# Third stage in two product runs per block, half-block cosine, and wider spacing of the weight splits: retention, routed experts and a cosine feed-forward on one core

## The chip, the cores and the metric

One core of one Trainium2 chip runs the whole program. The metric is the device time of one execution in microseconds (us); lower is better.

## The reference

```python
# stage 1: retention over 8 batches, 8 heads, 576 positions, head size 64
ret = (scale * q @ k.T) * Dmat          # Dmat: gamma ** (row - column), lower triangle
x = (ret @ v) laid out as 4608 tokens x 512
# stage 2: 8 experts, one per token
e = argmax(x @ w_gate);  x = gate_w * (relu(x @ w1[e]) @ w2[e])    # 512 -> 1024 -> 512
# stage 3
h = x @ w_in                            # 512 -> 2048
out = (h * cos(h)) @ w_out              # 2048 -> 512
```

All inputs are random; `w_in` and `w_out` arrive as 64-bit floats and are turned into 32-bit ones on the chip.

## The kernel before

An fp32 product is made of three passes of rounded operands: each operand is split into a rounded part (a copy on ScalarE, ACT) and a rest (a subtraction on VectorE, DVE), and TensorE (PE) multiplies high by high, low by high and high by low. The program has three stages; every engine executes its instructions in the order in which the Python code emits them.

**Stage 2, the experts** (lines 595 to 881). Each of 8 experts has room for 616 tokens, in two halves of 256 and 360 columns. A half has 12 groups of matmuls: eight of the first layer (`layer1`, line 646, 12 matmuls each, evicted by ACT at line 649 and DVE at line 650) and four of the second (`layer2`, line 661, 24 matmuls each, evicted by ACT at line 663). Six PSUM banks (`hps`) turn over between them. After each group the loop calls `step_bg` (line 855), which advances a background generator by one or two turns (a turn ends at a `yield`), and `step_bgs`, which splits half a weight tile of the next expert. The background generator is `conv` (line 690): 32 tiles of the stage-3 weights are loaded, turned into 32-bit floats on DVE (seven turns, lines 700 to 712), split by `split_out` (line 681: an ACT copy into a buffer `cvo` of which there are two, a turn, a DVE subtraction, and two DMAs from GpSimd, POOL, to scratch memory in HBM) and stored. For `w_in`, four tiles together go to `combine` (line 724), which forms seven combined quarter matrices (a fast 2x2 scheme with seven products instead of eight) and splits and stores each (`keep`). There are four such combines. In the last expert the stage-3 weights are read back by `wide_unit` (eight loads of 1 MB) and `ws_load`, on the SP queue.

**Between the stages** stands `tc.If(late > 0)` (line 979) for overflowing experts, not taken here. All engines pass it together, and SP first waits for the DMAs that it has issued.

**Stage 3** (lines 987 to 1181). Nine tiles of 512 tokens; each tile has eight steps (a pair of 128-wide blocks of the hidden layer each), 72 steps `i` in all. A step has seven quarter products (`product`, line 1043, six matmuls of 256 columns each), whose inputs are seven combinations of input quarters (`turned`, line 1019, makes four of them; `enter`, lines 1026 and 1028, splits all seven). `decode` (lines 1057 and 1060) adds the products up to four quarters of h, `gate` (lines 1070 to 1083) turns each quarter of 128x256 into h cos h and splits it, and `down` (line 1113) multiplies by `w_out`: 24 matmuls of 512 columns per step, into four accumulators `acc`. After the last step of a tile `leave` evicts the four accumulators, alternately on DVE and ACT, into one of three row buffers, and POOL writes the rows out by an indirect DMA. The loop at line 1149 emits, per product, three or four matmuls of `down` of the step before (`PIECE`), so the 256- and 512-column matmuls alternate in seven pieces per step. `ahead` says at which points the next tile's inputs are loaded, turned and split.

Of the kernel before, what the change touches and what calls it, by code (L numbers as in the profile page):

```python
# [11 lines left out]
F32 = mybir.dt.float32  # L12
# [91 lines left out]
def attn_moe_kernel(ctx, tc, q, k, v, wg, w1, w2, win, wout, ctab, out):  # L104
# [490 lines left out]
    with ExitStack() as mctx:  # L595
# [128 lines left out]
        def combine(g, kc):  # L724
# [12 lines left out]
            yield from keep(4, n)  # L737
            sub(out=n, in0=n, in1=a11)
            yield
            yield from keep(1, n)  # L740
            yield from keep(2, a12)
            sub(out=a12, in0=a12, in1=n)
            yield
            yield from keep(6, a12)
# [80 lines left out]
        for e in range(E):  # L825
# [7 lines left out]
            for i, (hf, l, k) in enumerate(work):  # L833
# [21 lines left out]
                step_bg(2 if l == 2 or k % 2 == 1 else 1)  # L855
# [10 lines left out]
                elif i % 3 == 2:  # L866
                    wide_unit((0, 2, 1, 3)[i // 6], i // 3 % 2, nc.sync)
# [3 lines left out]
                if e + 1 == E and i in (17, 21):  # L871
                    ws_load(i // 21)
# [124 lines left out]
    near = yp.tile([P, 3, 2, 2, HT], F32R, name="near")  # L997
    ring += [near[:, n] for n in range(3)]
# [15 lines left out]
    def turned(T, n):  # L1014
# [4 lines left out]
        nc.vector.tensor_sub(out=t, in0=a, in1=b)  # L1019

    def enter(T, n, half=(0, 1)):
        src = [part(T, 0, 0), turn.get((T, 2)), part(T, 1, 0), turn.get((T, 3)), turn.get((T, 1)), turn.get((T, 4)),
               part(T, 1, 1)][n]
        t = enc[T, n] = ring[(NSLOT * T + n) % len(ring)]
        if 0 in half:
            nc.scalar.copy(out=t[:, 0], in_=src)
        if 1 in half:
            nc.vector.tensor_sub(out=t[:, 1], in0=src, in1=t[:, 0])

    BANK = (0, 1, 0, 1, 2, 3, 2)  # L1030
    SEEN = (0, 0, 1, 1, 0, 0, 1)
    bank = {}

    def product(i, s):
        T, q = i // NQ, i % NQ
        if not SEEN[s]:
            bank[i, BANK[s]] = psA.tile([P, 512], F32, tag="h", name="hps", bufs=4)
        o = bank[i, BANK[s]][:, :HT]
        u, x = units[2, i], enc[T, s]
        idx = 0  # L1040
        for kc in range(2):
            for a, bq in ((0, 0), (1, 0), (0, 1)):
                mm(out=o, lhsT=u[:, s, kc, a], rhs=x[:, bq, kc], start=(idx == 0 and not SEEN[s]), stop=(idx == 5),  # L1043
# [3 lines left out]
    h = {}  # L1047

    def decode(i, s):
        o = bank[i, BANK[s]][:, :HT]  # L1050
        if s == 2:
            h[i, 0, 0] = o
            return
        t = gp.tile([P, HT], F32, tag=f"d{s}", name="part", bufs=1 if s < 4 else 2)
        h[i, s] = t
        if s == 0:
            nc.scalar.copy(out=t, in_=o)  # L1057
            return
# [151 lines left out]
```

## Time and profile before

| | before |
|---|---|
| median of 3 runs | 1511.27 us (1510.29 to 1511.37) |
| the profiled execution | 1513.19 us, span 1511.4 us |
| PE matmul busy | 1444.5 us (96%) |
| DVE busy, ACT busy | 986.7 us (65%), 776.4 us (51%) |
| mean granted TensorE clock | 0.98 |
| stage 1 / stage 2 / stage 3 start | 0 / about 235 us / about 722 us |

The profile shows one execution: busy time of each engine, what ended each idle time, a time line, and for any stretch the busy time and the granted clock. PE is busy nearly throughout, so time is lost where PE waits, where its clock is lowered, and in the spacing of matmuls that follow one another without a wait. A busy matmul's duration includes its latency; the spacing is read from start to start.

### The profile page before, as it was taken

Reading aid. Unit: us, or ns where it says so; the run is one execution under the profiler, and the core shown is the slowest. Engines: PE = TensorE matmul, PEld = TensorE weight load, DVE = VectorE, ACT = ScalarE, POOL = GpSimd, SP = SyncE. Lnnn points to the kernel's source line nnn. Section 1 sums busy time; section 2 is a strip of 40 time slices with the busy share of each in tenths; the row PEclk is TensorE's granted clock in tenths of the full one; section 3 lists DMA queues with packets and bytes.
Section 4 is the critical chain, followed back from the end, with each engine's and each line's share of the span. In section 5 each row is a group of like instructions: output and inputs, shape, how many; then the busy total and the mean of one; then the engine's idle time right before and its main releaser. Section 6 shows DMA issues by size and latency. Waiting matters only on the chain.

```text
span 1511.4 us, 29804 instructions
## 1 busy us (share of the span) xinstructions
PE 1444.5 (96%) x11591; PEld 1330.9 (88%) x11591; DVE 986.7 (65%) x2321; ACT 776.4 (51%) x1911; POOL 223.0 (15%) x335
## 2 busy tenths in 40 slices
PE   8999979989999998999699999999999999999998
PEld 7888868989999998999698898989898898988887
DVE  3677666576766666741676766767677676767665
ACT  2344423434444534532466666666666665656654
POOL 3242532303210412210001001010100001010101
PEclk9999988999999999999799999999999999999999
DMA  9898936567665767766445555464646455555542
GB/s 189 207 218 213 221 99 178 184 190 230 199 212 181 231 196 223 227 208 242 151 175 216 183 194 207 163 242 156 249 152 225 173 204 196 190 209 189 190 180 77
DMA packets 179938, 293.48 MB, mean 194 GB/s; under 512 B 120676, under 2 KB 129328, under 8 KB 169552
## 3 DMA queue, kind: packets, MB, share of 16 engines
q1 hardware_dynamic: 166672, 248.92, 52.0%
q0 software_dynamic: 13120, 42.61, 8.4%
q8 instruction: 92, 1.51, 0.4%
q14 instruction: 54, 0.44, 0.1%
HBM read 239.43 MB, written 52.06 MB: 193 GB/s over the span
## 4 chain that ended last, share of the span: by engine, by line
PE 29%; issue 15%; ACT 3%; DMA 3%; DVE 2%; POOL 0%; POOLq 0%; DVEq 0%; ACTq 0%
PE acc L1113 15%; PE hps L1043 14%; DMA out_dram<-orow,perm 3%; ACT sa L1074 1%; ACT sa L1075 1%; ACT ka L1070 0%; ACT orow L1095 0%; DVE sa L1072 0%; ACT gh L1081 0%; POOL out_dram L1097 0%; DVE sa L1077 0%; DVE gl L1083 0%; DVE orow L1093 0%; ACT part L1057 0%; DVE turn L1019 0%
## 5 line engine op out<-in xcount | busy, mean ns | idle before, releaser
L1113 PE MATMUL acc<-wunit,gh 128*128 128x512 f32 x1152 | 395.4, 395 | 0.0
L1043 PEld LDWEIGHTS hps<-far,wquad 128*128 128x128 f32 x2160 | 306.2, 190 | 39.4 <-ACT part L1057 10.1
L1043 PE MATMUL hps<-far,wquad 128*128 128x256 f32 x2160 | 317.4, 283 | 5.0 <-ACT part L1057 4.9
L1060 DVE TENSOR_TENSOR part<-hps,part 128x256 f32<-128x256 f32 x360 | 152.2, 423 | 120.0 <-PE hps L1043 115.3
L1113 PEld LDWEIGHTS acc<-wunit,gh 128*128 128x128 f32 x1152 | 208.1, 189 | 23.3
L646 PE MATMUL hps<-xT,wunit 128*128 128x360 f32 (+1 forms) x1536 | 223.1, 306 | 4.7 <-DVE hl L650 4.7
L1113 PE MATMUL acc<-wunit,gl 128*128 128x512 f32 x576 | 227.4, 395 | 0.0
L646 PEld LDWEIGHTS hps<-xT,wunit 128*128 128x128 f32 x1536 | 220.2, 190 | 5.8 <-DVE hl L650 5.4
L661 PE MATMUL hps<-hh,wunit 128*128 128x360 f32 (+1 forms) x1024 | 223.6, 310 | 0.9 <-ACT hh L649 0.8
L1074 ACT ACTIVATE sa<-sa 128x256 f32<-128x256 f32 x288 | 120.5, 418 | 181.3 <-DVE sa L1072 181.3
L661 PEld LDWEIGHTS hps<-hh,wunit 128*128 128x128 f32 x1024 | 171.7, 192 | 1.3 <-ACT hh L649 1.3
L661 PE MATMUL hps<-hl,wunit 128*128 128x360 f32 (+1 forms) x512 | 158.4, 309 | 5.6 <-DVE hl L650 5.6
L1081 ACT CAST gh<-sa 128x256 fp32r<-128x256 f32 x288 | 117.1, 407 | 77.9 <-DVE sa L1077 77.9
L1097 POOL DMA_INDIRECT out_dram<-orow,perm x36 | 35.1, 974 | 801.9 <-DVE orow L1093 547.3
L1043 PEld LDWEIGHTS hps<-near,wquad 128*128 128x128 f32 x864 | 123.2, 191 | 28.8 <-ACT part L1057 9.9
L1083 DVE TENSOR_TENSOR gl<-sa,gh 128x256 fp32r<-128x256 f32 x288 | 121.4, 421 | 34.5 <-ACT gh L1081 25.4
L1043 PE MATMUL hps<-near,wquad 128*128 128x256 f32 x864 | 128.5, 285 | 14.6 <-ACT part L1057 7.7
L777 DVE TENSOR_TENSOR wunit<-wst,wunit 128x512 fp32r<-128x512 f32 x112 | 75.7, 686 | 79.8 <-ACT wunit L776 79.7
L1077 DVE SCALAR_TENSOR_TENSOR sa<-sa,part 128x256 f32<-128x256 f32 x216 | 91.9, 425 | 53.2 <-ACT sa L1075 46.0
L1075 ACT ACTIVATE sa<-sa 128x256 f32<-128x256 f32 x288 | 120.3, 418 | 9.2
L1113 PEld LDWEIGHTS acc<-wunit,gl 128*128 128x128 f32 x576 | 109.3, 190 | 10.2
L661 PEld LDWEIGHTS hps<-hl,wunit 128*128 128x128 f32 x512 | 98.3, 192 | 8.4 <-DVE hl L650 8.4
(178 smaller groups left out, 1815.6 us busy)
## 6 DMA issues: line engine op xcount, KB each, us to landing
wquad<-ws SPq DMA_DIRECT2D x72, 1792.0 KB, 7.4
wst<-in_moe_w_dram SPq DMA_DIRECT2D x64, 512.0 KB, 5.2
ws<-cvo POOLq DMA_DIRECT2D x56, 256.0 KB, 4.5
ldq<-in_q_dram SPq DMA_DIRECT2D x32, 256.0 KB, 4.6
ldk<-in_k_dram SPq DMA_DIRECT2D x32, 256.0 KB, 5.3
ldv<-in_v_dram SPq DMA_DIRECT2D x32, 256.0 KB, 5.3
xd<-xs SPq DMA_DIRECT2D x32, 256.0 KB, 3.0
cvw<-in_moe_w_in_dram SPq DMA_DIRECT2D x16, 512.0 KB, 4.8
```

The lines of the kernel that those rows point to most:

```text
L646: mm(out=ph[:, :n], lhsT=u[:, a, kc, f0:f0 + P], rhs=t[:, bq, kc, :n], start=(idx == 0), stop=(idx == 11))
L661: mm(out=py[:, :n], lhsT=u[:, w], rhs=t[:, :n], start=(fc == 0 and g == 0), stop=(fc == 7 and g == 2))
L777: nc.vector.tensor_sub(out=u[:, 1, 2 * g + c], in0=s[:, c], in1=u[:, 0, 2 * g + c])
L1043: mm(out=o, lhsT=u[:, s, kc, a], rhs=x[:, bq, kc], start=(idx == 0 and not SEEN[s]), stop=(idx == 5), skip_group_check=True)
L1060: nc.vector.tensor_add(out=t, in0=o, in1=h[i, other])
L1074: nc.scalar.activation(out=sa, in_=sa, func=AF.Sin, scale=math.pi)
L1075: nc.scalar.activation(out=sa, in_=sa, func=AF.Square, scale=math.sqrt(2.0))
L1077: nc.vector.scalar_tensor_tensor(out=sa, in0=sa, scalar=-1.0, in1=x, op0=ALU.add, op1=ALU.mult)
L1081: nc.scalar.copy(out=gh, in_=sa)
L1083: nc.vector.tensor_sub(out=gl, in0=sa, in1=gh)
L1097: ins = nc.gpsimd.indirect_dma_start(out=out[:, :], out_offset=bass.IndirectOffsetOnAxis(ap=perm[:, k:k + 1], axis=0), in_=o, in_offset=None)
L1113: mm(out=acc2[T][c], lhsT=t[:, c % 2 * P:(c % 2 + 1) * P], rhs=u[:, w, fc % 4], start=(q == 0 and fh == 0 and n == 0 and w == 0), stop=(q ...
```

## The change

Five edits in two stages.

```diff
@@ stage 2: combine and the background turns
             def keep(k, x):
                 yield from split_out(x, ...)
+                yield
+                yield
...
-                step_bg(2 if l == 2 or k % 2 == 1 else 1)
+                step_bg(4 if l == 2 else 1)
...
-                elif i % 3 == 2:
+                elif i % 3 == 0:
                     wide_unit((0, 2, 1, 3)[i // 6], i // 3 % 2, nc.sync)
...
-                if e + 1 == E and i in (17, 21):
-                    ws_load(i // 21)
+                if e + 1 == E and i in (16, 20):
+                    ws_load(i // 20)
@@ stage 3: inputs
-    near = yp.tile([P, 3, 2, 2, HT], F32R, name="near")
+    near = yp.tile([P, 5, 2, 2, HT], F32R, name="near")
-        nc.vector.tensor_sub(out=t, in0=a, in1=b)
+        (eng or nc.vector).tensor_tensor(out=t, in0=a, in1=b, op=ALU.subtract)
...
-    turned(0, 1)
...
+    turned(0, 1, nc.gpsimd)
...
+    turned(0, 2, nc.gpsimd)
...
+    turned(0, 3, nc.gpsimd)
...
+    turned(0, 4, nc.gpsimd)
@@ stage 3: sums and cosine, two quarters at a time
+    def decode_a(i):
...
+        nc.scalar.copy(out=p1, in_=x[:, :HT])
+        nc.vector.tensor_add(out=u2, in0=y[:, :HT], in1=p1)
+        nc.vector.tensor_add(out=u3, in0=z[:, HT:], in1=u2)
+
+    def decode_b(i):
...
+        nc.scalar.copy(out=t[:, 0], in_=x[:, :HT])
+        nc.vector.tensor_add(out=t[:, 1], in0=x[:, HT:], in1=u3)
+        nc.vector.tensor_add(out=p1, in0=y[:, :HT], in1=p1)
+        nc.vector.tensor_add(out=t[:, 2:4], in0=z.rearrange("p (a t) -> p a t", a=2),
+                             in1=p1.unsqueeze(1).to_broadcast([P, 2, HT]))
...
-        ka = gp.tile([P, HT], I32, tag="ka", name="ka", bufs=3)
+        ka = gp.tile([P, 2, HT], I32, tag="ka", name="ka", bufs=2)
@@ stage 3: the loop
+        if i < NALL:
+            for n in range(4):
+                product(i, n)
+            decode_a(i)
+        advance()
+        more(i, 1)
+        if i >= 2:
+            down(i - 2, 1)
+        advance()
+        more(i, 2)
+        if i < NALL:
+            for n in range(4, NSLOT):
+                product(i, n)
+            decode_b(i)
+        advance()
+        if i < NALL:
+            active.append(((i, 0), gate(i, 0)))
+        more(i, 3)
         if i + 2 < NALL:
             ws_load(i + 2)
+        if 1 <= i <= NALL:
+            down(i - 1, 0)
+        advance()
+        if i < NALL:
+            active.append(((i, 1), gate(i, 1)))
+        more(i, 4)
```

`advance` moves every active `gate` by two of its six turns; a `gate` now works on a pair of quarters (128x512 per instruction), and `down(i, half)` has the 12 matmuls of half the columns. `turned` takes an engine; for the first tile it is GpSimd. The seven quarter matrices and inputs are renumbered, so that four products run first and three second; three PSUM banks hold a step instead of four. A step's matmuls are the same in number and shape.

In the first of the four combines ACT is the engine that is waited for. `L684` is the copy into a `cvo` buffer, `L776` the split of the next expert's weights (`L778` after), `L663` and `L649` the evictions of the second and the first layer. Before:

```order
L649 ACTIVATE hh<-hps 128x360 x2
L684 CAST cvo<-cvn 128x512
L776 CAST wunit<-wst 128x512
L631 CAST xT<-tp 128x4x128 x2
L663 COPY yev<-hps 128x360
L684 CAST cvo<-cvn 128x512
L684 CAST cvo<-cvm 128x512
L776 CAST wunit<-wst 128x512
L663 COPY yev<-hps 128x360
L684 CAST cvo<-cvm 128x512
L663 COPY yev<-hps 128x360
L684 CAST cvo<-cvm 128x512 x2
```

The change, at the end of the same combine:

```order
L663 COPY yev<-hps 128x360
L684 CAST cvo<-cvm 128x512 x2
L778 CAST wunit<-wst 128x512 x3
...
L649 ACTIVATE hh<-hps 128x256
L618 ACTIVATE xrow<-xrow,sgate 128x512
L649 ACTIVATE hh<-hps 128x256
L618 ACTIVATE xrow<-xrow,sgate 104x512
L649 ACTIVATE hh<-hps 128x256
L684 CAST cvo<-cvm 128x512
```

The seven copies into the two buffers reach from the first layer of one half into the first layer of the next, where they took one second layer and its edges before.

On SP, in the last expert, the loads of `w_out` (`L785`, after `L787`) stand between the stores of the second layer (`L665`). Before, up to the branch:

```order
L665 DMA ydT<-yev 128x360
L790 DMA wquad<-ws_74 128x3584
L665 ISA
L665 DMA ydT<-yev 128x360
L665 ISA
L665 DMA ydT<-yev 128x360
L785 DMA wunit<-wd_73 128x2048
L979 COMPARE_AND_BRANCH
```

The change:

```order
L792 DMA wquad<-ws_74 128x3584
L665 ISA
L665 DMA ydT<-yev 128x360
L787 DMA wunit<-wd_73 128x2048
L665 ISA
L665 DMA ydT<-yev 128x360
L665 ISA
L665 DMA ydT<-yev 128x360
L981 COMPARE_AND_BRANCH
```

The last 1 MB load is issued two groups earlier, and the last DMA ahead of the branch is a store.

In stage 3, at the end of a tile, ACT in the change (`L1098` evicts an accumulator, `L1084` rounds a pair of quarters, `L1053` copies the first product, `L1073` to `L1078` are the cosine):

```order
L1098 ACTIVATE orow<-acc_10713 128x512
L1073 ACTIVATE ka<-quad 128x512
L1053 COPY part<-hps 128x256
L1077 ACTIVATE sa<-sa 128x512
L1078 ACTIVATE sa<-sa 128x512
L1073 ACTIVATE ka<-quad 128x512
L1098 ACTIVATE orow<-acc_10773 128x512
L1084 CAST gh<-sa 128x512
L1077 ACTIVATE sa<-sa 128x512
```

The fourth accumulator's eviction now stands right ahead of the rounding that the next run of `down` needs; before, the copy of the first product stood four narrow instructions behind the second eviction, and twelve behind the fourth.

## Rows read from the trace of the kernel before

**Rows 1.** Stage 2 by half experts: stretch, length, engines' busy us, clock, DMA, GB/s.

```profile
449.10:481.70 32.60, 32.60 (x202) 32.58 (x201) 20.32 (x39) 12.96 (x26) 3.58 (x4) 1.00 0.61 199
481.70:505.80 24.10, 24.10 (x206) 23.94 (x205) 18.55 (x35) 12.22 (x27) 6.51 (x8) 1.00 0.56 168
294.00:327.20 33.20, 27.74 (x205) 26.51 (x204) 22.39 (x44) 13.02 (x29) 7.85 (x9) 0.90 0.69 214
359.80:392.00 32.20, 27.62 (x207) 26.61 (x206) 22.06 (x44) 13.44 (x30) 8.36 (x11) 0.89 0.67 232
563.50:601.80 38.30, 33.95 (x202) 32.49 (x201) 22.94 (x43) 15.86 (x32) 11.44 (x15) 1.00 0.76 241
```

**Rows 2.** Waits of the whole run: who waits for whom, us, times, longest.

```profile
ACT cvo L684 <- DMA ws<-cvo: 39.3, 17, 5.0
```

**Rows 3.** DMA issues: queue, count, KB each, median us from issue to landing.

```profile
ws<-cvo POOLq DMA_DIRECT2D x56, 256.0 KB, 4.5
```

**Rows 4.** Time line of the fourth combine: start, us, engine, line, what [idle before <-releaser].

```profile
571.64 1.49 POOL L688 DMA_DIRECT2D ws<-cvo  x2 [1.24 <-ACT cvo L684]
...
576.39 0.62 ACT L684 CAST cvo<-cvm 128x512 fp32r<-128x512 f32 x1 [5.04 <-DMA ws<-cvo]
...
578.75 0.92 PE L646 MATMUL hps<-xT,wunit 128*128 128x360 f32 x4 [3.12 <-DVE hl L650]
```

**Rows 5.** Time line of SP ahead of stage 3.

```profile
715.62 0.34 SPq L665 DMA_DIRECT2D ydT<-yev  x1
716.13 0.33 SPq L785 DMA_DIRECT2D wunit<-wd  x1
```

**Rows 6.** SP's own waits between 690 and 760 us.

```profile
SPq L979 <- SPq L979: 5.1, 4, 3.4
```

**Rows 7.** Time line: first instructions of ACT and DVE in stage 3.

```profile
722.19 0.62 ACT L1026 CAST near<-yfirst 128x512 fp32r<-128x512 f32 x1 [6.59 <-SPq L979]
722.30 0.69 DVE L1019 TENSOR_TENSOR turn<-yfirst 128x512 f32<-128x512 f32 x1 [22.01 <-SPq L979]
```

**Rows 8.** First 23 us of stage 3: PE and weight loads of L1043, then of L1113.

```profile
722.80:746.08 23.28, 15.05 (x78) 13.72 (x78) 0.68 0.39 126
722.80:746.08 23.28, 1.84 (x6) 1.52 (x7) 0.68 0.39 126
```

**Rows 9.** POOL's subtractions and products of two inputs, by shape, and one in the time line.

```profile
L423 POOL TENSOR_TENSOR hot<-hot,ge 128x200 f32<-128x200 f32 x7 | 7.5, 1077 | 0.6
...
L423 POOL TENSOR_TENSOR hot<-hot,ge 128x80 f32<-128x80 f32 x1 | 0.4, 356 | 0.1
...
205.72 0.61 POOL L423 TENSOR_TENSOR hot<-hot,ge 128x200 f32<-128x200 f32 x1
```

**Rows 10.** Two steps of stage 3, between tiles: the first undisturbed, the second not.

```profile
982.06:992.61 10.55, 10.55 (x67) 9.50 (x67) 6.42 (x16) 5.96 (x17) 0.00 (x0) 1.00 0.75 275
992.61:1003.91 11.30, 10.81 (x67) 9.41 (x66) 7.07 (x19) 6.76 (x19) 4.24 (x8) 1.00 0.72 254
```

**Rows 11.** Waits of the whole run: PE on ACT's copy of the first product.

```profile
PE hps L1043 <- ACT part L1057: 12.6, 17, 3.5
```

**Rows 12.** Time line: a tile's first row store, the weight load, the fourth eviction.

```profile
992.61 11.64 SPq L790 DMA_DIRECT2D wquad<-ws  x2
...
992.64 0.97 POOL L1097 DMA_INDIRECT out_dram<-orow,perm  x1 [75.63 <-DVE orow L1093]
...
1000.86 0.60 ACT L1095 ACTIVATE orow<-acc 128x512 f32<-128x512 f32 x1 [2.08 <-PE hps L1043]
```

**Rows 13.** Time line of PE: twelve narrow matmuls, a piece of three, the tail.

```profile
735.76 1.60 PE L1043 MATMUL hps<-near,wquad 128*128 128x256 f32 x12
...
1002.31 0.40 PE L1113 MATMUL acc<-wunit,gh 128*128 128x512 f32 x1
...
1003.01 0.88 PE L1043 MATMUL hps<-far,wquad 128*128 128x256 f32 x6
...
1498.52 0.39 PE L1113 MATMUL acc<-wunit,gl 128*128 128x512 f32 x1
...
1500.56 0.39 PE L1113 MATMUL acc<-wunit,gl 128*128 128x512 f32 x1
```

More of the change, by code (lines that the diff above doesn't have):

```diff
@@ L996, in attn_moe_kernel @@
     ring = []
-    near = yp.tile([P, 3, 2, 2, HT], F32R, name="near")
-    ring += [near[:, n] for n in range(3)]
+    near = yp.tile([P, 5, 2, 2, HT], F32R, name="near")
+    ring += [near[:, n] for n in range(5)]
     for m in range(2):
@@ L1100, in leave, with down @@
         disjoint(ins.ins, "out")
-    def down(i):
+    def down(i, half):
         T, q = i // NQ, i % NQ
-        for c in range(4):
+        if q == 0 and half == 0:
+            acc2[T] = {}
+        pair = G.pop((i, half))
+        for c in (2 * half, 2 * half + 1):
+            if q == 0:
+                acc2[T][c] = psA.tile([P, DM], F32, tag=f"acc{c}", name=f"acc{c}")
             for fh in range(2):
@@ L1109, in down @@
                 for n, w in ((0, 0), (0, 1), (1, 0)):
-                    if q == 0 and c == 0 and fh == 0 and n == 0 and w == 0:
-                        acc2[T] = [psA.tile([P, DM], F32, tag=f"acc{k}", name=f"acc{k}") for k in range(4)]
-                    t = G[i, fh, c // 2][n]
-                    mm(out=acc2[T][c], lhsT=t[:, c % 2 * P:(c % 2 + 1) * P], rhs=u[:, w, fc % 4],
+                    mm(out=acc2[T][c], lhsT=pair[n][:, fh, c % 2 * P:(c % 2 + 1) * P], rhs=u[:, w, fc % 4],
                        start=(q == 0 and fh == 0 and n == 0 and w == 0), stop=(q == NQ - 1 and fh == 1 and n == 1))
-                    if q == NQ - 1 and fh == 1 and n == 1:
-                        leave(T, c)
-                    yield
-        for k in ((0, 0), (0, 1), (1, 0), (1, 1)):
-            del G[(i,) + k]
+            if q == NQ - 1:
+                leave(T, c)
     NB = NT // P
@@ new lines, in attn_moe_kernel, with advance @@
+    turned(0, 4, nc.gpsimd)
+    for n in (2, 3, 5):
+        enter(0, n)
+    ahead = {(0, 2): [raw_load], (1, 2): [turned, 1], (1, 4): [turned, 2], (2, 2): [turned, 3], (2, 4): [turned, 4],
+             (3, 2): [enter, 0], (3, 4): [enter, 1], (4, 2): [enter, 2], (4, 4): [enter, 3], (5, 2): [enter, 4],
+             (5, 4): [enter, 5], (7, 3): [enter, 6]}
+    active = []
+    def advance():
+        for _, g in active:
+            next(g)
+        for _, g in active:
+            next(g)
+        active[:] = [(k, g) for k, g in active if k not in G]
@@ new lines, in more @@
+    def more(i, point):
+        T, q = i // NQ, i % NQ
+        if T + 1 < NTILE and (q, point) in ahead:
+            f = ahead[q, point]
+            f[0](T + 1, *f[1:])
+    for i in range(NALL + 2):
+        if i < NALL:
[16 more added lines that the diff above has]
+        more(i, 3)
```

117 lines of the change are left out of this document (34 added, 83 removed).

## The prediction

> **What bounds the kernel.** I read the page's busy times first: PE is busy 96% of the span, so a gain has to come from PE's gaps, its clock or its spacing. The windows view by half experts shows where stage 2 loses: an undisturbed half takes 24.1 us (256 columns) or 32.6 us (360 columns), three others take 33.2, 32.2 and 38.3 us for the same matmuls, two of them with the granted clock at 0.90 and 0.89, so partly at the lower level of 1.2 GHz [rows 1]. That is 9.1 + 8.1 + 5.7 = 22.9 us. The view of waits names what is late there: ACT waits 39.3 us in 17 pieces until the stores of the split weights have freed a `cvo` buffer [rows 2]. The time line shows such a piece: ACT stands 5.04 us ahead of a copy, the evictions behind it are late, and PE, out of PSUM banks, waits 3.12 us [rows 4]. Stage 3 is PE from end to end: an undisturbed step takes 10.55 us with PE busy all of it [rows 10]. It loses time at its start [rows 7, 8] and at the end of each tile [rows 10, 11].
>
> **Stage 2: the splits.** Before, a combine is 11 turns (four sums, seven copies), and a half expert gives 20 turns (12 in its first layer, 8 in its second), so the seven splits are asked for in about half a half, 12 to 16 us. A buffer is taken for the copy 0.62, the subtraction 0.69, as another of the same width [rows 7], two POOL issues 1.49 [rows 4] and the landing 4.5 us [rows 3]: 7.3 us. Two buffers give a split per 3.65 us, seven in 25 us. The missing 10 us is what ACT stands still per combine: 39.3 / 4 = 9.8. After, a combine is 11 + 14 = 25 turns and a half gives 8 + 16 = 24, so the seven splits are asked for in about one half, 24 to 33 us. Demand meets supply. Within that, a second layer takes 16 turns, 5.3 splits, in 12 to 16 us and wants 19: ACT will still stand 3 to 4 us there. What covers that is the second layer itself: one short eviction per group and six PSUM banks. If that cover fails, the three slow halves come back in part. DVE gets four turns at once in a second layer (sixteen of up to 0.69 [rows 7], with the other splits and the transposed inputs more than a 12 us layer holds); it may run 2 to 3 us late into a first layer that has the banks to bear it. I take 21.5 of the 22.9 us as gained. The bounds: all of it, 23, and 8, if the landing under load is nearer 7 us than 4.5.
>
> **The branch.** The last 1 MB load is issued at 716.13 [rows 5], and SP waits at the branch, 3.4 us in its longest piece [rows 6], before ACT starts at 722.19 [rows 7]. With that load two groups of the second layer earlier the last thing in flight is the store of 715.62 [rows 5]; the 3.4 us piece goes: **-3.4 us**. It is nothing if another load lands as late, at best a little more.
>
> **The first step.** The first 84 matmuls of stage 3 (78 narrow, 6 wide) take 23.3 us [rows 8], where the steady spacing (below) would need 78 x 0.119 + 6 x 0.2325 = 10.7; 12.6 us are lost, to ACT and DVE preparing the inputs and to a clock of 0.68. Now POOL makes the four turned inputs, one after the other. Its price for 128x512: by the undisturbed row 0.61 at 200 columns and 0.356 at 80, so 2.1 ns a column, 1.26 us; by the mean 1.077 of all seven [rows 9], 6 ns a column, 2.95 us. The rows with the larger time are those that a DVE instruction with two SBUF inputs overlaps, and they are longer by about that overlap. I take 1.3 us each plus the DVE subtractions that fall into it (0.69 each, three in the first, one in each other), so the four are ready 3.4, 5.4, 7.5 and 9.5 us after the release. The last split and the copy of the first product follow ACT's order: 10.5 us. Then 18 narrow matmuls at the low level, 256 columns at 1.2 GHz or 0.213 us each: the first step ends 14.3 us after the release, 13.7 after the first matmul, 8.7 over its 5.0 at full rate. From there I find no stall: the second step has 42 more products before the first `down`. So 12.6 becomes 8.7 or a little more: **-3.5 us**. Bounds: -5 (clock up earlier), +3 (2.95 us each). The Trainium skill (GPSIMD Engine Reference, sections 1 and 4.1) speaks against this edit: elementwise work with two inputs belongs on VectorE, GpSimd being about 2x slower and sharing SBUF interfaces with it. The trace agrees on both counts (0.61 at 200 columns, 1.077 with overlap); by its 4497 ns for 2048 columns a turn would cost an estimated 1.1 us, and the sum would be the same within 1 us.
>
> **The tile ends.** At eight tile changes ACT's copy of the first product comes late behind the evictions: 17 waits, 12.6 us, of which 6.0 in the first step, so 15 of 0.44 us [rows 11], each with a restart. A disturbed step is 0.75 us longer [rows 10]. Between 6.6 (idle alone) and 15 x 0.75 = 11.3 I take 9 us. After, that copy has a run of 12 wide matmuls to hide behind, but the fourth eviction now stands ahead of the rounding for the next `down`, and it waits for the tile's first row store, which took 8.2 us (992.64 to 1000.86) beside a weight load issued in the same instant [rows 12]. Take t = 0 at the end of the first half of `down`. PE then has 24 narrow matmuls (to 2.85), 12 wide (to 5.65) and 18 narrow (to 7.8). The tile's first accumulator is done at -1.4 and its store starts near -0.2; the weight load, released by the narrow run before, starts at -2.8. So the store starts 2.6 us behind the load instead of with it, and I expect it done near 6. The fourth accumulator is ready at 5.65, its eviction ends near 6.7, the rounding near 7.4, and PE wants that at 7.8; where the store is a little later, PE waits. A stall of 0.3 us on average, 2.5 in all: **-6.5 us**. Bounds: -9, and +4 if the store takes its 8.2 us (1.65 us at each end).
>
> **The spacing.** Six narrow products take 0.71 us, 0.1185 each; in a piece of three the wide ones take (1003.01 - 1002.31) / 3 = 0.233, and in the tail, with nothing between, (1500.56 - 1498.52) / 9 = 0.2267 [rows 13]. By the step, (10.55 - 42 x 0.1185) / 24 = 0.232 [rows 10]. So 24 wide matmuls in seven pieces cost 0.14 us more than in one; with two pieces 2/7 of it stays: -0.10 us, 72 times, -7. Long narrow runs cost (1.60 - 0.28) / 11 = 0.120 [rows 13], 42 x 0.0010 x 72 = +3. I take **-4 us**, between -7 and +3. The Trainium skill (TensorE: Matmul & The Clock Gate, Back-to-back issue gap) gives a warm matmul N/2.4 + 2.5 ns alone, whatever stands beside it: then this term is 0. The trace shows 0.2267 and 0.233 for the same shape, so neighbours count.
>
> **The pair width.** ACT and DVE work per step falls (a 128x512 instruction takes 0.60 [rows 12] and 0.69 [rows 7], two of 128x256 about 0.8), which is worth nothing, since PE is the bound. What it must not do is come late: see the third rival.
>
> **The sum.** -21.5 - 3.4 - 3.5 - 6.5 - 4 = -38.9. The profiled execution took 1513.2 us, 1.9 over the median: 1474.3 by profile, **1472.4 us** by the median.
>
> **Rivals.**
> First, the splits still hold ACT: a landing of 7 us makes 9.8 us per buffer, 34 us for seven splits, more than a half. DMA at 0.67 to 0.76 in the slow halves [rows 1] speaks for it, the longer stretch against. Stage 2 then gives 8: 1486 us.
> Second, the fourth eviction: the store takes as long as before, PE waits 1.65 us per tile end, +4 instead of -6.5: 1483 us. The weight load's head start speaks against it.
> Third, slower: the pairs come late in every step. A pair's chain starts at the fourth product's end, 2.85 us after t = 0, and takes a narrow sum (under 0.69), a DVE pass 0.69, the rounding 0.60 and the rest 0.69, so with handoffs it ends near 5.9; PE wants the rest at 8.3, two wide matmuls into its run. That leaves 2.4 us. If the queues ahead of it on ACT and DVE eat that and 0.54 us more, the 38.9 us are gone; 1 us over gives 72 - 38.9 = +33: 1544 us. DVE and ACT at about 60% in a step [rows 10] speak against it.
> Fourth, spacing follows the shape alone (the page's rule): the term is 0, 1476 us.
> Fifth, the change doesn't do what it says: some other copy or load holds SP and ACT as now, and only the tile ends and spacing are left, -10: 1501 us.
>
> **How the numbers follow.** The forecast's own case 0.55, with the fourth rival 0.2 inside the same range; the first 0.1, the second 0.08, the third 0.03, the fifth 0.04. The range takes the forecast's bounds (-23 - 3.4 - 5 - 9 - 7 = -47, 1464) a little widened, 1462, up to just over the first rival, 1488. A measurement of this kernel can tell about 0.2%, 3 us. Faster 0.95; same 0.02 and slower 0.03 come from the third rival and part of the fifth.
>
> **What would show it.** ACT's wait for stored splits falls from 39.3 to under 15 us, and every half expert but the first takes under 25 or 34 us. The first product of stage 3 starts about 3.9 us after SP issues its last store instead of 7.2. POOL's turns take 1.3 to 3.4 us. No PE wait on the copy of the first product after the second step; waits at tile ends, if any, on the rounding `gh`. Wide matmuls at 0.228 on average. I am wrong if slow halves remain, if PE waits once per step, or if a step is over 10.55 us.

## The result, and the profile after

The changed kernel takes 1468.8 us (median of 4 runs, 1467.5 to 1470.0) against 1511.3 us of the kernel before beside it: a ratio of 0.970, interval 0.966 to 0.975. The profiled execution took 1467.5 us, its span is 1465.7 us against 1511.4 us. Forecast were 1472.4 us, in a range of 1462 to 1488 us.

The stages below compare one traced execution of each kernel. That of the kernel before was 1.9 us over its median, that of the changed kernel 1.3 us under, so the traces are 45.7 us apart where the medians are 42.5.

By stage, from first and last matmuls (us; "first two steps" are part of stage 3, which includes the spacing and the tile ends):

| | before | after | difference | forecast |
|---|---|---|---|---|
| start of stage 2 | 235.5 | 235.2 | -0.3 | 0 |
| stage 2 | 479.6 | 453.6 | -26.0 | -21.5 |
| last product of stage 2 to first of stage 3 | 7.80 | 3.76 | -4.0 | -3.4 |
| stage 3, all | 782.9 | 766.1 | -16.7 | -14.0 |
| its first two steps | 24.86 | 20.50 | -4.4 | -3.5 |
| over the median step at 8 tile ends | 10.9 | 0.5 | -10.4 | -6.5 |
| median step | 10.55 | 10.52 | -2 over 70 steps | -4 |
| behind the last matmul | 5.7 | 7.0 | +1.3 | 0 |

Both kernels have 84 narrow matmuls in their first two steps, the changed one 12 wide ones with them and the kernel before 10.

Stage 2 by half experts, the columns as in [rows 1]: the first half, one that was slow before (294.0 to 327.2 there) with the next, and a late pair.

```profile
235.20:260.90 25.70, 25.70 (x205) 25.48 (x205) 21.80 (x54) 9.79 (x22) 4.83 (x4) 0.93 0.64 197
...
293.50:317.50 24.00, 24.00 (x207) 24.00 (x206) 17.66 (x35) 12.61 (x28) 7.57 (x9) 1.00 0.80 257
317.50:350.10 32.60, 32.60 (x203) 32.58 (x202) 22.01 (x40) 13.98 (x28) 6.97 (x8) 1.00 0.58 177
519.80:543.70 23.90, 23.90 (x205) 23.90 (x205) 18.65 (x35) 12.32 (x27) 4.89 (x6) 1.00 0.57 178
543.70:576.30 32.60, 32.60 (x202) 32.58 (x201) 19.48 (x35) 15.42 (x31) 12.37 (x16) 1.00 0.76 243
```

PE is busy in every half from end to end, also where the DMA engines are busy 0.80 of the time; no slow half is left but the first, which has its granted clock at 0.93. The waits say why; this row answers to [rows 2], 39.3 us in 17 pieces:

```profile
ACT cvo L684 <- DMA ws<-cvo: 10.3, 6, 3.3
```

The time line of the changed kernel from the last store of stage 2 through the first step of stage 3, SP, ACT, POOL, DVE and PE (start, us, engine, line, what [idle before <-releaser]):

```profile
689.34 0.34 SPq L665 DMA_DIRECT2D ydT<-yev  x1
...
691.86 1.66 ACT L1027 CAST near<-yfirst 128x512 fp32r<-128x512 f32 x3 [2.55 <-SPq L981]
691.97 1.27 POOL L1021 TENSOR_TENSOR turn<-yfirst 128x512 f32<-128x512 f32 x1 [49.49 <-SPq L981]
692.51 4.65 DVE L1028 TENSOR_TENSOR near<-yfirst,near 128x512 fp32r<-128x512 f32 x3 [18.51 <-ACT near L1027]
692.53 0.80 PE L1043 MATMUL hps<-near,wquad 128*128 128x256 f32 x2 [2.09 <-ACT near L1027]
693.32 1.60 POOL L1021 TENSOR_TENSOR turn<-yfirst,turn 128x512 f32<-128x512 f32 x1
...
696.57 1.71 POOL L1021 TENSOR_TENSOR turn<-yfirst,turn 128x512 f32<-128x512 f32 x1
...
697.08 1.75 DVE L1028 TENSOR_TENSOR far<-turn,far 128x512 fp32r<-128x512 f32 x1
698.75 1.28 DVE L1028 TENSOR_TENSOR near<-turn,near 128x512 fp32r<-128x512 f32 x2
...
699.48 3.63 PE L1043 MATMUL hps<-near,wquad 128*128 128x256 f32 x16 [2.31 <-DVE near L1028]
```

SP's last issue is now a store, not a load, and ACT starts 2.52 us behind it ([rows 5, 7]: 722.19 - 716.13 = 6.06). SP's longest wait at the branch, 3.4 us in [rows 6], is 0.6 us (view of SP's waits, 670 to 740 us: us, times, longest):

```profile
SPq L981 <- SPq L981: 1.5, 3, 0.6
```

Then comes something of which the forecast had only one half. It had POOL slowed by DVE; DVE is slowed by POOL as well. DVE's first four subtractions take 1.27, 1.76, 1.76 and 1.75 us, each beside one of POOL's, and the last three 0.68 each, once POOL is done. The first three in the view of the line (ns: shortest, median, longest):

```profile
L1028 DVE TENSOR_TENSOR near<-yfirst,near x3: 1275/1761/1762, 692.5 to 695.4; 128x512 fp32r<-128x512 f32 x3
```

The last PE wait of the step, 2.31 us, is for DVE. The first two steps, and a step at a tile end, in the windows view:

```profile
692.53:704.39 11.86, 9.00 (x43) 8.12 (x44) 9.07 (x10) 4.02 (x8) 5.67 (x4) 0.57 0.32 91
704.39:713.03 8.64, 8.29 (x58) 7.20 (x56) 7.34 (x15) 6.17 (x11) 0.00 (x0) 1.00 0.85 294
955.15:965.67 10.52, 10.52 (x68) 9.54 (x66) 6.38 (x12) 6.94 (x13) 4.17 (x8) 1.00 0.75 276
```

The third row stands against the disturbed step of [rows 10], 11.30 us with PE busy 10.81. PE now works through this tile's end. The spacing, in PE's own time line there:

```profile
955.15 3.04 PE L1043 MATMUL hps<-far,wquad 128*128 128x256 f32 x24
958.02 0.63 PE L1118 MATMUL acc<-wunit,gh 128*128 128x512 f32 x2
...
960.77 0.88 PE L1043 MATMUL hps<-far,wquad 128*128 128x256 f32 x6
```

Twelve wide matmuls take 960.77 - 958.02 = 2.75 us, 0.229 each; 24 narrow ones 2.87 us, 0.1196 each.

### The profile page after: what moved, and what is told of

It reads as the page before. It is cut to its first block, busy times and chain, and to the rows that moved or that the text cites. A ratio compares the mean times of both kernels' runs of the same rounds, so it can differ in the third digit from the quotient of the medians.

```text
span 1465.7 us, 28943 instructions
## 1 busy us (share of the span) xinstructions
PE 1427.4 (97%) x11591; PEld 1327.4 (91%) x11591; DVE 959.6 (65%) x1885; ACT 718.1 (49%) x1407; POOL 230.3 (16%) x339
## 4 chain that ended last, share of the span: by engine, by line
PE 46%; issue 5%; DMA 1%; POOL 0%; DVE 0%; ACT 0%; POOLq 0%; ACTq 0%
PE acc L1118 24%; PE hps L1043 22%; DMA wquad<-ws 1%; POOL out_dram L1100 0%; DVE near L1028 0%; DVE far L1028 0%; POOLq L1216 0%; ACT ka L1073 0%; ACT near L1027 0%; POOL spare L141 0%; ACTq L1027 0%; POOLq L1100 0%; ACT orow L1098 0%
## 5 line engine op out<-in xcount | busy, mean ns | idle before, releaser
L1118 PE MATMUL acc<-wunit,gh 128*128 128x512 f32 x1152 | 358.3, 392 | 0.0
L1043 PEld LDWEIGHTS hps<-far,wquad 128*128 128x128 f32 x1824 | 231.7, 191 | 6.2
L1043 PE MATMUL hps<-far,wquad 128*128 128x256 f32 x1824 | 236.5, 283 | 0.0
L1043 PE MATMUL hps<-near,wquad 128*128 128x256 f32 x1200 | 161.6, 286 | 5.3 <-DVE near L1028 2.8
L1043 PEld LDWEIGHTS hps<-near,wquad 128*128 128x128 f32 x1200 | 156.6, 195 | 11.2 <-DVE near L1028 3.7
L1080 DVE SCALAR_TENSOR_TENSOR sa<-sa,quad 128x512 f32<-128x512 f32 x144 | 99.0, 688 | 42.9 <-ACT sa L1078 41.9
L1084 ACT CAST gh<-sa 128x512 fp32r<-128x512 f32 x144 | 89.5, 621 | 72.9 <-DVE sa L1080 72.9
L1086 DVE TENSOR_TENSOR gl<-sa,gh 128x512 fp32r<-128x512 f32 x144 | 99.0, 687 | 20.7 <-ACT gh L1084 15.2
L1054 DVE TENSOR_TENSOR part<-hps,part 128x256 f32<-128x256 f32 x72 | 30.6, 424 | 121.3 <-PE hps L1043 118.3
L1075 DVE SCALAR_TENSOR_TENSOR sa<-quad,ka 128x512 f32<-128x512 f32 x144 | 98.9, 687 | 12.2 <-ACT ka L1073 12.2
L663 ACT COPY yev<-hps 128x256 f32<-128x256 f32 (+1 forms) x64 | 26.6, 416 | 148.4 <-issue 77.9
L650 DVE SCALAR_TENSOR_TENSOR hl<-hps,hh 128x360 fp32r<-128x360 f32 (+1 forms) x128 | 60.5, 476 | 56.3 <-ACT hh L649 55.6
```

The costliest lines, as they stand in the source:

```text
L650: nc.vector.scalar_tensor_tensor(out=hl[:, :n], in0=ph[:, :n], scalar=0.0, in1=hh[:, :n], op0=ALU.max, op1=ALU.subtract)
L663: nc.scalar.copy(out=y[:, :n], in_=py[:, :n])
L1043: mm(out=o, lhsT=u[:, s, kc, a], rhs=x[:, bq, kc], start=(s in (0, 1, 2) and idx == 0), stop=(idx == 5), skip_group_check=True)
L1054: nc.vector.tensor_add(out=u2, in0=y[:, :HT], in1=p1)
L1075: nc.vector.scalar_tensor_tensor(out=sa, in0=x, scalar=INV2PI, in1=ka, op0=ALU.mult, op1=ALU.subtract)
L1080: nc.vector.scalar_tensor_tensor(out=sa, in0=sa, scalar=-1.0, in1=x, op0=ALU.add, op1=ALU.mult)
```

## The experiments

The lengths of stages below are measured as in the table. All kernels but the seventh start from the changed one.

**1. The old pace of the splits.**

```diff
-                yield
-                yield
...
-                step_bg(4 if l == 2 else 1)
+                step_bg(2 if l == 2 or k % 2 == 1 else 1)
```

> The changed kernel with the pace of the splits in the experts' stage as it was: two or one background steps after every unit, and no spare turns between two splits. Theory (two stores of split weights in flight hold ScalarE, so that the next split waits in front of the evictions): all of the stage's gain goes, the stage lengthens from 453.6 to about 479.6 us, the slow half experts are back at 27 to 28 and 34 to 35 us, ScalarE's wait for a free split buffer is back from 10.3 to about 39 us, and the time is 1468.8 + 26 = 1494.8 us (1491 to 1498). Rival (part of the 26 us came from something else, a first half or the time at which the stage starts): the stage lengthens by less than 20 us.

Stage 2 takes 476.4 us, 22.8 more than in the changed kernel, and the time is 1491.4 us (ratio to before 0.985, 0.984 to 0.987). The wait (first fence, from the view of waits) and the slow halves (second fence, one of them by windows, with the clock at 0.89) are back:

```profile
ACT cvo L684 <- DMA ws<-cvo: 39.1, 16, 5.0
```

```profile
359.80:391.30 31.50, 27.33 (x206) 26.23 (x205) 21.98 (x44) 13.43 (x30) 8.35 (x11) 0.89 0.67 224
```

So the pace carries 22.8 of the 26.0 us. The other 3.2 us lie almost wholly in one half expert (33.2 us in the kernel before [rows 1], 30.7 here), in which both kernels emit the same instructions but for the places that the stores go to; what it comes from stays open. In run 7, whose stage 2 is that of the kernel before, stage 2 takes 478.8 us and this half 32.5, so about 0.8 of the 3.2 us lies between two executions.

**2. The new pace without the spare turns.**

```diff
-                yield
-                yield
```

> The changed kernel without the two spare turns behind each split, and with the new pace (four background steps after a unit of layer 2, one after a unit of layer 1). In layer 2 a split then comes about every 0.9 us, in layer 1 every 1.9 us, so that two in flight cover 1.9 and 3.8 us of a store's 4.5 us. Theory (the distance between splits is what counts, wherever they stand): ScalarE's wait for a free split buffer is back at 25 to 60 us, and the stage loses 10 to 26 us. Rival (what counts is that layer 1, whose roundings the products of layer 2 wait for, is left alone; a wait in layer 2 costs nothing): the wait is back as well, but the stage loses 0 to 4 us.

Stage 2 takes 473.3 us, 19.7 more, the time is 1488.5 us, and ACT waits 32.1 us for buffers. Layer 1 is left alone here as in the changed kernel, so the rival falls: the distance between the splits counts. In this kernel the crowd is passed on in a second way, too. In POOL's queue the gather of the next expert's rows stands behind four store issues, and ACT's scaling of those rows behind the gather (time line of one such place):

```profile
299.60 2.98 POOL L688 DMA_DIRECT2D ws<-cvo  x4 [5.61 <-ACT cvo L684]
...
302.88 1.04 POOL L611 DMA_INDIRECT xrow<-xd,sid  x1 [0.30 <-PE hps L646]
...
308.24 0.72 ACT L618 ACTIVATE xrow<-xrow,sgate 104x512 f32<-104x512 f32 x1 [3.54 <-DMA xrow<-xd,sid]
...
309.45 4.39 PE L646 MATMUL hps<-xT,wunit 128*128 128x256 f32 x24 [5.20 <-DVE hl L650]
```

**3. The spare turns with a level pace.**

```diff
-                step_bg(4 if l == 2 else 1)
+                step_bg(3 if l == 2 else 2 if k % 2 == 1 else 1)
```

> The changed kernel with the spare turns, but with the background steps nearly level over the units: three after a unit of layer 2, and two or one in turn after a unit of layer 1 (24 for a half expert, as in the changed kernel). A split then comes about every 3.7 us in both layers, two in flight cover 7 us. Theory (the distance between splits counts): the stage stays within 3 us of the changed kernel's 453.6 us and ScalarE's wait for a free split buffer stays under 12 us. Rival (layer 1 has to be left alone): the stage loses 8 to 26 us though the wait for the split buffer stays small.

Stage 2 takes 455.8 us, 2.2 more (the other kernels with the changed kernel's stage 2 lie between 452.5 and 454.0), ACT's wait is 7.9 us, the time 1470.0 us. Runs 2 and 3 together: with the spare turns it hardly matters in which layer the splits run, and without them the choice of the layer doesn't help.

**4. The loads of the last expert in their old places.**

```diff
-                elif i % 3 == 0:
+                elif i % 3 == 2:
...
-                if e + 1 == E and i in (16, 20):
-                    ws_load(i // 20)
+                if e + 1 == E and i in (17, 21):
+                    ws_load(i // 21)
```

> The changed kernel with the loads of stage 2's last expert back in the old places (down weights at every third place from the third on, the combined weights' loads after units 17 and 21), so that SyncE issues its last transfers later. Theory (the instruction that decides the branch waits until SyncE has issued everything before it, and its last loads come after the last rows are stored): the stretch from the last product of the experts to the first of the quarter products is 7.2 to 7.8 us again instead of 3.76, and the time is 1468.8 + 3.8 = 1472.6 us (1471.5 to 1474). Rival (the 4 us come from the rows' stores that end earlier with the new pace): the stretch stays under 5 us and the time does not change.

The stretch is 7.90 us, the time 1473.0 us. SP's time line shows the load behind the last store, and 6.13 us until SP is past the branch:

```profile
692.70 0.33 SPq L787 DMA_DIRECT2D wunit<-wd  x1
698.83 0.34 SPq L1124 DMA_DIRECT2D permT<-idc  x1
```

SP's longest wait at the branch is 4.0 us here (view of SP's waits, 670 to 740 us):

```profile
SPq L981 <- SPq L981: 5.1, 3, 4.0
```

**5. The first tile's subtractions on DVE.**

```diff
-    turned(0, 1, nc.gpsimd)
+    turned(0, 1)
```

(the same for 2, 3 and 4)

> The changed kernel with the first tile's four subtractions of inputs on VectorE again, in the changed kernel's order. In the changed kernel VectorE's own subtractions (0.68 us alone) took 1.55 and 1.75 us while GpSimd ran a subtraction beside them, and the last split was ready 11.2 us after SyncE's last store. Theory A (the two engines hinder each other, so GpSimd's help is worth little, and the first step gained from the order in which the splits are entered): on VectorE eleven subtractions of 0.69 us one behind another are 7.6 us, the first two steps of stage 3 take between 1 us less and 1 us more than the changed kernel's 11.86 + 8.64, and the time stays within 1.5 us of 1468.8 us. Theory B (GpSimd's help is worth the 3.5 us that were predicted): the first two steps are 2.5 us longer or more, 1471.5 us or over.

The first two steps take 10.49 + 8.64 = 19.13 us, 1.4 less than in the changed kernel, and the time is 1464.1 us (1463.3 to 1466.5). The seven traces that share the changed kernel's start of stage 3 (the changed kernel and runs 1 to 4, 8 and 11) have 20.4 to 21.6 us there, so 19.1 lies clear of them. POOL's help, which the change brought and the forecast credited, is a loss; theory B falls, and A was still too kind to POOL: the steps and the time are both below what it allowed. Two of the groups of DVE's eleven subtractions, in the first 11 us after the branch (us in all, mean ns):

```profile
L1028 DVE TENSOR_TENSOR near<-yfirst,near 128x512 fp32r<-128x512 f32 x3 | 2.1, 687 | 18.4 <-ACT near L1027 18.4
L1021 DVE TENSOR_TENSOR turn<-yfirst,turn 128x512 f32<-128x512 f32 x2 | 1.4, 685 | 0.0
```

In the changed kernel the four of POOL and the four of DVE beside them fill 691.97 to 698.83 = 6.9 us; here seven and four on one engine take from 690.36 to 697.07, 6.7 us. The median is 4.7 us lower than that of the changed kernel, more than stage 3 gives (1.5 us). The two traced executions are 3.6 us apart, and the other 2.1 us of that say nothing about this edit: stage 2 starts 1.1 us earlier, and it is 1.0 us shorter because its first half ran at a granted clock of 1.00 and not 0.93.

**6. TensorE kept busy until the first split.**

```diff
-NWARM3 = 8
+NWARM3 = 26
```

> The changed kernel with 26 matmuls of no use instead of 8 between the branch and the quarter products, so that TensorE is busy until the first split is there; the granted clock was 0.57 in the first step of stage 3. Theory A (the first step pays for the low clock: behind the last wait, from 699.48 to 704.4 us, it runs 24 to 30 matmuls at about twice their time): the granted clock of the first step rises over 0.8, the step is 2 to 3 us shorter, and the time is 1466 to 1467 us. Rival (the waits for the splits bring the clock down again, or the splits alone set the step's end): the step is shorter by less than 1 us and the time does not change.

The first step of this kernel in the windows view:

```profile
692.23:703.89 11.66, 7.83 (x43) 7.13 (x44) 9.07 (x10) 4.01 (x8) 5.67 (x4) 0.71 0.33 94
```

The clock of the first step is 0.71, the step is 0.2 us shorter, the next 0.4 us; the time is 1467.7 us. That the 26 matmuls raised the clock is not shown: in the seven traces with 8 of them and the same start of stage 3 it lies between 0.51 and 0.71. The rival holds: as long as DVE and POOL are late, the clock decides little. Run 2 shows it, too, with a clock of 0.71 and a first step of 11.91 us, against 0.57 and 11.86 in the changed kernel.

**7. The kernel before with four row buffers.**

```diff
-    rowp = ctx.enter_context(tc.tile_pool(name="rowp2", bufs=3))
+    rowp = ctx.enter_context(tc.tile_pool(name="rowp2", bufs=4))
```

> The kernel before with four buffers instead of three for the rows that leave, so that no eviction of a finished accumulator waits for a row's store. At its eight tile ends two steps in a row were disturbed, the first 0.74 us and the second 0.6 us over 10.55 us. Theory (the first is late by the work of an eviction ahead of the copy of the first product on ScalarE, the second because ScalarE's last eviction waited 2 us for a row's store and pushed the roundings behind it back): the second step of each pair falls to 10.55 us, the first stays, stage 3 is about 4.6 us shorter than 782.85 us, and the time is 1511.3 - 4.6 = 1506.7 us. Rival (both are the work of the evictions): both stay, 1511.3 us. Second rival (both come from the row's store): both go, 1501 us.

The two steps at one tile end of this kernel in the windows view:

```profile
993.06:1004.37 11.31, 10.82 (x68) 9.42 (x67) 7.65 (x20) 7.47 (x20) 3.78 (x8) 1.00 0.73 256
1004.37:1014.92 10.55, 10.55 (x67) 9.47 (x66) 7.09 (x18) 6.66 (x19) 0.00 (x0) 1.00 0.50 175
```

At all eight tile ends the second step falls to 10.55 or 10.56 us and the first stays at 11.25 to 11.31. Stage 3 is 778.0 us, 4.9 shorter; the time is 1508.7 us against 1510.9 of the kernel before beside it, a ratio of 0.998 (0.997 to 1.000). Before, then, two causes of about 5 and 6 us stood side by side: an eviction that waited for a row's store, and an eviction's work ahead of the copy of the first product.

**8. Four pieces instead of two.** `down` is called for one `c` at a time, in four places of the step: between the second and third product, behind the fourth, behind the fifth and at the end.

```diff
-    def down(i, half):
+    def down(i, c):
...
+            for n in range(2):
+                product(i, n)
+        if i >= 2:
+            down(i - 2, 1)
```

> The changed kernel with the 24 wide matmuls of a step in four pieces of six instead of two of twelve (and the narrow ones in runs of 12, 12, 6 and 12); the work is the same. In the changed kernel the first five wide matmuls of a piece took 233, 236, 228, 233 and 231 ns and the rest 227, and the first two narrow ones of a run 113 and 119 ns and the rest 120. Theory (each piece costs what its first matmuls are longer, 26 ns, less the 8 ns that a narrow run's first are shorter): two more pieces make a step 0.04 us longer, 10.56 us, and the stage 2 to 3 us longer. Rival (spacing is by shape alone): 10.52 us, no change. Second rival (shorter pieces bring waits with them, as seven pieces did): some steps are over 10.7 us and TensorE waits at tile ends.

One step, measured from one wide piece's start to the same one's in the next step, in the windows view:

```profile
960.17:970.74 10.57, 10.57 (x69) 9.54 (x68) 6.55 (x13) 5.59 (x11) 2.09 (x4) 1.00 0.72 271
```

Every step from the fourth on takes 10.56 us, at the tile ends too, and stage 3 is 3.6 us longer, 2.8 of it in the steps; rival and second rival fall. (The kernel was run once, 1479.5 us; its stage 2 started 8 us later than the changed kernel's, so the time as a whole tells nothing.) But seven pieces (10.55) were no worse than four. By the traces of the three kernels, from start to start, a piece's wide matmuls take 233, 236, 228, 233 and 231 ns and then 227, and the pieces of three of the kernel before 236, 234 and 227. So the extra falls on a piece's first five matmuls: a piece of three pays 16 ns, one of four 21, one of six or twelve 26, and the theory's price holds from two pieces to four but not for seven. Against it go the narrow matmuls, which got slower with longer runs (0.1185 us in [rows 13], 0.1196 now).

**9 and 10. The splits of the first tile in the order of the products,** on DVE; in run 10 with 26 idle matmuls, too.

```diff
     enter(0, 0)
-    turned(0, 1, nc.gpsimd)
+    turned(0, 1)
     enter(0, 1)
...
+    turned(0, 2)
+    turned(0, 3)
+    enter(0, 2)
+    enter(0, 3)
+    turned(0, 4)
+    enter(0, 4)
+    enter(0, 5)
     enter(0, 6)
...
```

> The changed kernel with the first tile's four subtractions of inputs on VectorE, and with the splits entered in the order in which the products ask for them (so far 0, 1, 4, 6, 2, 3, 5), each subtraction ahead of the split behind it. By 0.61 us for one VectorE instruction behind another the split for the third product is then ready 3.6 us after the first starts and the last 6.7 us after it. Theory A (in the first step the 42 narrow matmuls at the low clock, 0.213 us each or 8.9 us, are the bound, and the wait for the splits shrinks from 1.74 to about 1 us): the first step takes 9.6 to 10 us where it was 10.49 with the old order of entry and 11.86 in the changed kernel, and the time is 1463.3 to 1464.5 us. Rival (the order of entry hides a later wait, for the last split): 10.4 us or more, 1464 us or over.

> As the run before, with 26 matmuls of no use instead of 8 between the branch and the quarter products. Theory A (with shorter waits the clock stays up, and the splits, the last of them ready 6.7 us after the first product, set the end of the first step): granted clock over 0.85 in the first step, the step takes 7.8 to 8.8 us, and the time is 1462 to 1463.5 us. Rival (the short waits bring the clock down all the same): clock under 0.8, the step takes 9.3 us or more, and the time is that of the run before.

The first step of run 9, and then of run 10, in the windows view:

```profile
696.30:705.11 8.81, 7.50 (x43) 6.61 (x44) 7.75 (x14) 3.99 (x8) 0.00 (x0) 0.81 0.40 122
```

```profile
694.95:703.76 8.81, 6.41 (x42) 5.40 (x43) 7.75 (x14) 3.99 (x8) 0.00 (x0) 1.00 0.42 124
```

Both steps take 8.81 us, with the clock at 0.81 and at 1.00: with the clock up, PE only waits longer (busy 6.41 instead of 7.50 us). So run 9 beat its theory A, which had PE at the low clock throughout, and run 10 reached the clock of its theory A and stood just outside its 8.8. In both PE's last wait of the step, 1.20 us, is for ACT's copy of the first product, which ACT takes up behind the copies of the last splits. Stage 3 is 763.0 and 762.2 us. The times are 0.4 and 0.5 us over the two theories' ranges; 1464.9 and 1464.0 us (ratios 0.968, 0.966 to 0.971, and 0.968, 0.965 to 0.970) beat the kernel before, but their intervals overlap that of the changed kernel, so that they beat it, too, is read from stage 3 (3.2 and 3.95 us shorter; the changed kernel and runs 1 to 4, which share its stage 3, lie between 766.0 and 767.4), not from the times.

**11. Two row buffers.**

```diff
-    rowp = ctx.enter_context(tc.tile_pool(name="rowp2", bufs=3))
+    rowp = ctx.enter_context(tc.tile_pool(name="rowp2", bufs=2))
```

> The changed kernel with two buffers instead of three for the rows that leave, so that the third and the fourth eviction of a tile wait for the stores of its first and second row; this gives the second rival of the prediction (an eviction that waits for a row's store stands on ScalarE ahead of a rounding that TensorE wants) the wait that it lacked. At a tile end of the changed kernel the stores are issued at 956.06 and 957.32 us, the last evictions run at 959.76 and 960.97 us, the rounding at 961.46 us, and TensorE wants it at 962.9 us. Theory (a row's store takes about 5 us from its issue, the fourth eviction ends near 963 and the rounding near 963.6 us): TensorE waits about 1 us at each of eight tile ends, on the rounding or what follows it, stage 3 is 6 to 12 us longer than 766.12 us, and the time is 1475 to 1481 us. Rival (the stores land in time, or the run of 18 narrow matmuls covers it): under 2 us, 1468 to 1471 us.

A miss. ACT and DVE now wait for rows' stores 15 times, 25.0 us in all, and PE hardly notices: two tile ends are 0.46 and 0.98 us late, stage 3 is 1.0 us longer, the time 1471.5 us. The time line of one tile end of this kernel:

```profile
957.58 0.96 POOL L1100 DMA_INDIRECT out_dram<-orow,perm  x1 [76.50 <-issue]
...
962.09 0.69 DVE L1096 TENSOR_SCALAR orow<-acc 128x512 f32<-128x512 f32 x1 [0.73 <-DMA out_dram<-orow,perm]
...
962.69 0.60 ACT L1098 ACTIVATE orow<-acc 128x512 f32<-128x512 f32 x1 [2.14 <-DMA out_dram<-orow,perm]
...
963.19 0.61 ACT L1084 CAST gh<-sa 128x512 fp32r<-128x512 f32 x1
...
964.44 0.63 PE L1118 MATMUL acc<-wunit,gh 128*128 128x512 f32 x2
```

A store is back 4.5 us after its issue (957.58 to 962.09), the rounding ends at 963.80, and PE, 18 narrow matmuls long, wants it at 964.44. At the eight tile ends of this trace a tile's first store is back in 4.4 to 6.4 us; it is issued 2.65 to 3.5 us behind a weight load. The fourth, within 1 us of the next weight load, takes 8.0 to 9.0 us. The view of DMA issues has these for the first and the fourth store of this tile end:

```profile
out_dram<-orow,perm POOLq DMA_INDIRECT x1, 4.4
```

```profile
out_dram<-orow,perm POOLq DMA_INDIRECT x1, 8.4
```

## Why the prediction was right, and where it was not

**Stage 2** (-21.5 forecast, -26.0). The mechanism held as put: demand for two buffers over their supply, ACT standing ahead of evictions, and the cure is distance (runs 1 to 3). The wait that remains, 10.3 us, costs PE nothing, as the cover in the second layer promised. The size was off because I held back 1.4 us of the 22.9 found, and because small losses spread over the other halves, which I had not counted, went as well: of the 26.0 us 22.8 are the pace by run 1, 3.2 are open. The first rival is out: every half but the first is at 24.0 or 32.6 us (the last at 31.9).

**The branch** (-3.4, -4.0). Shown by run 4. The term was SP's longest wait of before, 3.4 us, now 0.6. What was left out is that the load was also issued behind the last store: from SP's last issue to ACT's start 3.54 us went (6.06 to 2.52), and that issue stood 0.51 us behind the store [rows 5].

**The first step** (-3.5, -4.4). Near in size, wrong in its step "now POOL makes the four turned inputs", and near in part by luck. I had POOL take 1.3 us plus the DVE subtractions that fall into it, about 2 us, and DVE go on at 0.69 us. The trace has POOL at 1.27 to 1.72 us, with the four ready 6.4 us after the release and not 9.5, and DVE at 1.27 to 1.76: each DVE subtraction ends 0.55 us behind POOL's (697.08 + 1.75 = 698.83; POOL's ended at 696.57 + 1.71 = 698.28). The Trainium skill (SBUF — State Buffer, Who interferes with whom) says that a VectorE instruction with two SBUF inputs and a GpSimd instruction that reads SBUF exclude each other, the one that starts first holding the ports to its end. The turns and sums above agree (6.9 us for eight on two engines, 6.7 for eleven on one). So the first step took 11.86 us and not 13.7; the second, where I found no stall, is 0.9 us over the spacing of its 42 narrow and 12 wide matmuls, and the two errors partly cancel. What the prediction quoted of the Trainium skill (GPSIMD Engine Reference, sections 1 and 4.1) spoke against this edit, and run 5 bears it out: 1.4 us lost. Run 5 keeps the whole gain without POOL, so the gain came from the rest of the change at this place: the order in which inputs are entered, and the products in two runs with their sums. Which of these gave how much was not tried; run 9 shows that a better order was worth another 1.7 us.

**The tile ends** (-6.5, -10.4). The step that failed is the fourth eviction's wait, "a stall of 0.3 us on average": what is left is 0.5 us at all ends together, and 0.42 of it at a single one. There the chain ran as forecast (time line of the changed kernel):

```profile
1298.43 0.60 ACT L1098 ACTIVATE orow<-acc 128x512 f32<-128x512 f32 x1 [2.72 <-PE acc L1118]
1298.93 0.61 ACT L1084 CAST gh<-sa 128x512 fp32r<-128x512 f32 x1
...
1299.59 0.73 PE L1118 MATMUL acc<-wunit,gh 128*128 128x512 f32 x2
```

The accumulator was done at 1297.57, and the eviction began at 1298.43, 6.55 us after the first row's store was issued; that it waited for this store is read from that gap, since the profile names the accumulator. At the other seven ends the eviction began 4.9 to 6.2 us after the first store's issue, and PE lost 0.1 us at most. I took the store to need 6.2 us at every end; in run 11 it needs 4.4 to 6.4, and even when evictions wait for it the run of 18 narrow matmuls covers most. The traces bear out that the weight load's head start shortens the store: 4.4 to 6.4 us there against 7.5 to 8.2 in the kernel before, where load and store were issued within 1 us of each other. The loss of before was 10.9 us, near my upper bound of 11.3 and not 9, since each tile end had two causes and not one (run 7). The second rival is out, and run 11 shows by how much.

**The spacing** (-4, -2). The mechanism held, the price of a piece did not. I let the 0.14 us of seven pieces fall to 2/7, 0.04; with 0.229 against 0.2267 of the tail [rows 13] two pieces still cost 24 x 0.0025 = 0.06 us, because a long piece pays 26 ns and a short one 16 to 21 (run 8), so that the cost does not go with the number of pieces. The narrow side came as taken, +0.046 us a step. The fourth rival (by shape alone) is out by run 8. The formula that the prediction quotes from the Trainium skill (TensorE: Matmul & The Clock Gate, Back-to-back issue gap) is given there for an isolated matmul; what neighbours do to the spacing it does not say.

**The pair width** and the third rival: from the fourth step on no step is over 10.52 us but one of 10.61 and one of 10.94, both at tile ends, so the pairs are not late. By the letter these two, and the third step with 10.59, are one of the prediction's signs of being wrong (a step over 10.55); together they are 0.6 us. That a pair is worth nothing in itself was not tried.

**The sum**: -38.9 forecast, -45.7 by the traces, -42.5 by the medians. Two terms went beyond the bounds that I gave them, stage 2 (23) and the tile ends (9); the spacing, -2 for -4, and the end behind the last matmul, +1.3, made up for a part of it. That end was not in the sum. It is the fourth eviction's wait once more, at the end of the last tile, where no matmuls follow that could cover it. The last eviction of the kernel before, and of the changed kernel (time lines):

```profile
1505.75 0.60 ACT L1095 ACTIVATE orow<-acc 128x512 f32<-128x512 f32 x1 [2.12 <-PE acc L1113]
```

```profile
1459.72 0.60 ACT L1098 ACTIVATE orow<-acc 128x512 f32<-128x512 f32 x1 [3.17 <-DMA out_dram<-orow,perm]
```

The first begins with the last matmul's end, the second 1.06 us behind it.

## What to carry to other kernels

Background work that ends in a store needs a distance between its pieces that is no shorter than the store's whole turn divided by its buffers; which phase it runs in matters much less. Before a second engine is given part of the work, look at whether the two read the same kind of operand beside each other: two engines that take turns are no faster than one. At the start of a stage, prepare inputs in the order in which they are asked for before you buy speed or clock; at its end, look for the run of other matmuls that covers a wait before you price the wait, and remember that behind the last tile there is none.

## What the runs showed of the hardware

- Subtractions of 128x512 with two SBUF inputs run beside each other on DVE and POOL took 1.27 to 1.76 us on DVE against 0.68 alone, and 1.60 to 1.72 us on POOL, whose first, begun alone, took 1.27; the forecast had only POOL slowed.
- The granted clock in the first step behind the branch was 0.51 to 0.71 in seven traces with 8 idle matmuls ahead of it, 0.71 in one with 26, 0.81 in one with 8 and shorter waits for the splits, and 1.00 in one with both; below 1.00 part of the step ran at 1.2 instead of 2.4 GHz. Between the last two the step's length did not change.
- A row's store of 256 KB was back 7.5 to 9.3 us after its issue when a weight load of 1.8 MB was issued within 1 us of it, 3.8 to 7.2 us when one was issued 2.6 to 4.8 us before, and 2.7 us at the end of the kernel, where none was near (kernel before and run 11).
- The spacing of matmuls depends on their place in a run, in opposite directions (changed kernel, medians from start to start): wide ones 0.227 us but for the first five behind narrow ones, 0.228 to 0.236; narrow ones 0.120 but for the first two behind wide ones, 0.113 and 0.119.
